# Three loads and one transposition moved along the queues of a fused sigmoid-attention and gated-FFN kernel

## The chip, the cores and the metric

The kernel runs on one core of a Trainium2 chip. The metric is the device time of one execution in microseconds (us). The time before is the median of three runs, 398.1 us (398.04 to 398.14).

## The reference

The inputs are `q`, `k` and `v` of shape (8 batches, 12 heads, 448 positions, 64) and three weight matrices. All are float32, and so is the output of 3584 rows of 768.

```python
scores = scale * np.matmul(q, k.transpose(0, 1, 3, 2)) - np.log(S)
attn = 1.0 / (1.0 + np.exp(-scores))          # a sigmoid, no sum over a row
x = np.matmul(attn, v)                        # then heads side by side: 3584 x 768
gate = np.maximum(x @ w_gate, 0.0)            # 768 -> 1536
out = (gate * (x @ w_val)) @ w_out            # 1536 -> 768
```

## The kernel before

**Tiling.** A batch has twelve heads, taken as three groups (g = 0, 1, 2) of four heads. The keys and queries of a group are held transposed in a tile `qkT`. The 448 positions are cut into seven chunks (c = 0 to 6). A *score unit* is one chunk of one group: `qk_unit` computes the scores on TensorE (L232) and their sigmoid on ScalarE (L187) into a tile `PT`. `pv_group` multiplies the seven `PT` tiles of a group by `v` (L250), and VectorE copies the result into `xT` (L184). The FFN of a batch follows: `gv` computes a gate block and a value block for each of twelve blocks f of 128 columns (L309), ScalarE or VectorE evicts the gate (L318, L320), and VectorE multiplies the two into `hT` (L327). Later FFN work is done for pairs of batches by sums of blocks (L385), which stay untouched.

**Order of TensorE.** It is written out by hand. Batches 1 to 7 have 21 score units each, cut into bursts m = 0, 1, 2 and so on. For batch 1 the bursts begin at units 0, 3, 6, 9, 13 and 17, and the `pv_group` of group 0 is in burst 3, that of group 1 in burst 5. The `pv_group` of group 2 stands in burst 0 of the next batch (`pv_finish`). Between bursts `ffn_mix(n)` takes n blocks off a queue of `gv` calls. During batch 1 these are still blocks of batch 0, whose positions are cut into two halves of 256 and 192: first the 192-wide blocks f = 0 to 5, then for f = 6 and 7, 8 and 9, 10 and 11 the 256-wide pair followed by the 192-wide pair.

**Loads.** `load` (L110), `load_v` (L114, L116), `load_gv` (L148) and `load_o` (L164) are all issued by GpSimd (POOL), one behind the other, and convert float32 to float16 on the way. Each transfer has one of eight semaphores in turn. A load so is not issued before the load eight places ahead of it has landed; the trace shows this as short POOL waits on DMAs. `k` and `q` of batches 2 to 7 share one buffer each, so the load of the next batch waits until the last group's copies (L215) have read the old one. `v` has two buffers in turn.

**Transposition.** Batches 0 and 1 are transposed on TensorE (`pe_transposes`, L201, L206). From batch 2 on `dma_transposes(b, g)` first has VectorE copy the group's `k` and `q` into a tile `rel` (L215, two instructions), and then SyncE (SP) issues a DMA transpose from `rel` to `qkT` (L219). `rel` has two buffers, so the third group's copies wait until the first group's transpose has landed. `qkT` has three.

**Where the changed steps stand.** `hold(b, g)` is a tiny copy on GpSimd (L646) that reads `qkT` of one group: POOL, and every load queued behind it, waits there until that transpose has landed. In burst 4 of batch 1 the first group of batch 2 is transposed; in burst 5, ahead of its two `gv` blocks, `late_loads` runs:

```python
4: [(3, lambda: dma_transposes(2, 0))],
5: [(2, late_loads)],
...
def late_loads():
    dma_transposes(2, 1)
    hold(2, 1)
    load_v(2)
    load_o()
```

The loads of batch 2's `k` and `q` are emitted in burst 0 of batch 1. Group 2 of batch 2 is transposed in burst 0 of batch 2, behind `pv_finish(1)`; in the same burst the loads of batch 3 are emitted. In the last burst of batch 2 the groups 0 and 1 of batch 3 are transposed, beside the first block of the down projection.

Of the kernel before, what the change touches and what calls it, by code (L numbers as in the profile page):

```python
# [17 lines left out]
def kernel(  # L18
# [75 lines left out]
    def tiles_of(b):  # L94
        if b not in in_tiles:
            pool = early if b == 1 else inp
            in_tiles[b] = tuple(
                p.tile([P, NPAIR, NCH * D], FP16, tag=t, name=t)
                for p, t in ((pool, "k16"), (pool, "q16"), (vinp, "v16"))
            )  # L100
        return in_tiles[b]

    def rows_of(src, b):
        return src[b].rearrange("(x r) (t c) d -> (r t) x (c d)", r=2, c=NCH)

    def load(b, g0, g1, which, c0=0, c1=NCH):
        for nm, t16, src in zip("kq", tiles_of(b), (k, q)):
            if nm in which:
                xs, cs = slice(2 * g0, 2 * g1), slice(c0 * D, c1 * D)
                nc.gpsimd.dma_start(t16[:, xs, cs], rows_of(src, b)[:, xs, cs])  # L110

    def load_v(b):
        v16 = tiles_of(b)[2]
        nc.gpsimd.dma_start(v16[:, 0::2, :], rows_of(v, b)[:, 0::2, :])  # L114
        for r in range(2):
            nc.gpsimd.dma_start(  # L116
                v16[64 - 64 * r : P - 64 * r, 1::2, :], rows_of(v, b)[64 * r : 64 * r + 64, 1::2, :]
            )
# [25 lines left out]
    def load_gv(f0, f1, which=(0, 1)):  # L144
        fs = slice(f0 * P, f1 * P)
        for i in which:
            wt, src = ((wg, moe_w_gate), (wv, moe_w_val))[i]
            nc.gpsimd.dma_start(wt[:, :, fs], src[:, fs].rearrange("(c p) f -> p c f", p=P))  # L148
# [6 lines left out]
    load(1, 0, 1, "kq")  # L155
    load_gv(6, 9)
    load(1, 1, 2, "kq")
    load_gv(9, 12)
    load_v(1)
    load(1, 2, 3, "kq")  # L160

    def load_o():
        for m0, m1 in ((0, 512), (512, DM)):
            nc.gpsimd.dma_start(  # L164
                wo[:, :, m0:m1], moe_w_out[:, m0:m1].rearrange("(c p) m -> p c m", p=P)
            )
# [23 lines left out]
    def qkT_of(b, g):  # L190
        if (b, g) not in qkT_tiles:
            qkT_tiles[(b, g)] = qkTp.tile([P, TW, P], FP16, tag="qkT", name="qkT")
        return qkT_tiles[(b, g)]
# [17 lines left out]
    def dma_transposes(b, g):  # L211
        k16, q16, _ = in_tiles[b]
        rel = relp.tile([P, TW, P], FP16, tag="rel", name="rel")
        for ti, t16 in enumerate((k16, q16)):
            nc.vector.tensor_copy(  # L215
                rel[:, ti * NCH : (ti + 1) * NCH, :].rearrange("p c (h d) -> p h c d", h=2),
                t16[:, 2 * g : 2 * g + 2, :].rearrange("p h (c d) -> p h c d", c=NCH),
            )
        nc.sync.dma_start_transpose(  # L219
            qkT_of(b, g)[:], rel[:].rearrange("p c x -> p (c x)")  # L220
        )
# [78 lines left out]
    def pv_group(b, g):  # L300
        pv(b, g, 0, S, [PT_tiles.pop((b, g, c))[:, :, 0:S] for c in range(NCH)])
# [66 lines left out]
    def open_late():  # L368
        first_sbuf.close()
        pool = ctx.enter_context(tc.tile_pool(name="late", bufs=1))  # L370
        late["T"] = pool.tile([P, 4, HF, HM], FP16, tag="T", name="T")
        late["X"] = pool.tile([P, 3, HD, S], FP16, tag="X", name="X")
        late["sums"] = ctx.enter_context(tc.tile_pool(name="sums", bufs=2))
# [21 lines left out]
    def weight_sums(i):  # L395
        T = [late["T"][:, j] for j in range(4)]
        B11, B21 = wo[:, 0:HF, 0:HM], wo[:, HF:NFC, 0:HM]
        B12, B22 = wo[:, 0:HF, HM:DM], wo[:, HF:NFC, HM:DM]
        sub(T[i], *((B12, B11), (B22, T[0]), (B22, B12), (B21, T[1]))[i])
# [96 lines left out]
    def batch_sums_t1(g):  # L496
        T1, _, _, B11, _, B12, _ = batch_blocks(g, (0, HD))
        sub(T1, B12, B11)

    def batch_sums(g, ks):  # L500
        T1, T2, T4, _, B21, B12, B22 = batch_blocks(g, ks)
        sub(B12, B22, B12)
        sub(T2, B22, T1)
        sub(T4, B21, T2)
# [132 lines left out]
    def pv_finish(b):  # L637
        pv_group(b, NG - 1)
        if b < 2:
            push_gv(b, 0, S, range(NFC))  # L640
# [4 lines left out]
    def hold(b, g):  # L645
        nc.gpsimd.tensor_copy(gate[0:1, :], qkT_tiles[(b, g)][0:1, 0, 0:2])  # L646

    def both(b, g):
        pe_transposes(b, g, 0)
        pe_transposes(b, g, 1)  # L650

    def late_loads():
        dma_transposes(2, 1)
        hold(2, 1)
        load_v(2)
        load_o()


# [2 lines left out]
    def push_group(g):  # L661
        tail = [("t", g, 6)] + [("y", g, p) for p in range(3)]
        if g == 0:
            tail.insert(0, tail.pop(1))
        work.extend([("w", g, f) for f in range(0, NFC, 2) if g > 0] + tail)
# [26 lines left out]
    for b in range(1, B):  # L692
        if b == 1:
            cuts, pv_at = (0, 3, 6, 9, 13, 17, 21), {3: (0, 2), 5: (1, 2)}
        elif b == 2:
            cuts, pv_at = (0, 4, 7, 11, 14, 18, 21), {0: (-1, 2), 2: (0, 2), 4: (1, 2)}
        else:
            cuts, pv_at = (0, 4, 8, 12, 16, 21), {0: (-1, 2), 2: (0, 2), 4: (1, 2)}
        count = len(cuts) - 1
        hooks = {}  # L700
        if b == 1:
            mix = (3, 3, 3, 3, 3, 2)
            hooks = {
                1: [(1, lambda: both(1, 1))],
                3: [(1, lambda: both(1, 2))],
                4: [(3, lambda: dma_transposes(2, 0))],
                5: [(2, late_loads)],
            }
        elif b == 2:
            mix = (2, 2, 1, 1, 1, 2)  # L710
            hooks = {
                2: [(0, prepare)],
                4: [(0, lambda: weight_sums(0))],
                5: [(1, lambda: weight_sums(1)), (0, lambda: weight_sums(2))],
            }
            open_late()
        elif b == 3:
            mix = (1, 1, 1, 0, 0)
        else:
            mix = (0,) * count  # L720
        for m in range(count):
            jobs = []
            for i, (g, c) in enumerate(order[cuts[m] : cuts[m + 1]]):
                if m in pv_at and i == pv_at[m][1]:
                    if m == 0:
                        pv_finish(b - 1)
                        if b == 2:
                            push_group(0)
                        elif b % 2 == 0:
                            push_group(b // 2 - 1)  # L730
                    else:
                        pv_group(b, pv_at[m][0])
                qk_unit(b, g, c)
            if m == 0 and b > 1:
                jobs.append(lambda: dma_transposes(b, 2))
            if b == 2 and m == count - 1:
                jobs.append(lambda: (dma_transposes(3, 0), dma_transposes(3, 1)))
            elif b == 3 and m == count - 1:
                jobs.append(lambda: (dma_transposes(4, 0), dma_transposes(4, 1)))
            elif 0 <= m - count + 2 and 3 < b < B - 1:  # L740
                jobs.append(lambda: dma_transposes(b + 1, m - count + 2))
            if b == 1:
                if m == 0:
                    load(2, 0, 1, "kq")
                    load(2, 1, 2, "kq")
                    load(2, 2, 3, "kq")
            elif m == 0 and b + 1 < B:
                if b == 3:
                    jobs.append(lambda: hold(3, 2))
                jobs.append(lambda: (load(b + 1, 0, 3, "kq"), load_v(b + 1)))  # L750
            if b % 2 and b > 2:
                if m == count - 1:
                    jobs.append(lambda: (batch_sums_t1(b // 2), batch_sums(b // 2, (0, 1))))
            elif b > 3 and m == 0:
                jobs.append(lambda: batch_sums(b // 2 - 1, (1, HD)))
            if b == 2 and m == count - 1:
                ffn_mix(mix[m], hooks[m])
                next_work(jobs + [lambda: weight_sums(3)], first_act=True)
            elif mix[m]:
                for job in jobs:  # L760
                    job()
                ffn_mix(mix[m], hooks.get(m, ()))
            else:
                next_work(jobs)
            if b == 3 and m in (1, 3):
                for f in range(*((0, 8, 2), (8, NFC, 2))[m // 2]):
                    gate_sums(f, f + 2)
# [35 lines left out]
```

## Time and profile before

| what | value |
|---|---|
| median of three runs | 398.1 us (398.04 to 398.14) |
| the profiled execution | 399.14 us |
| its span | 397.3 us |
| TensorE (PE) busy | 388.5 us, 98% of the span |
| ScalarE (ACT) busy | 223.2 us, 56% |
| VectorE (DVE) busy | 279.6 us, 70% |
| GpSimd (POOL) busy | 49.5 us, 12% |
| granted TensorE clock | 1.0 |

The span is the time from the first to the last instruction of the profiled execution; 1.84 us of that execution lie around it. Times in the views count from the start of the span. PE is the matrix engine, PEld its weight loads. The timeline merges like instructions that follow each other: a line gives the start, the length, the engine, the source line, the operation with its tiles, and a count; in brackets stands the idle time before it and what ended it. Successive matmuls overlap in the record, since their ends are modelled, so the distance between the starts of two lines says better than their lengths how long the first kept the engine.

### The profile page before, as it was taken

What the parts mean: (1) busy time and instruction counts of PE and PEld (TensorE: products, weight loads), DVE (VectorE), ACT (ScalarE), POOL (GpSimd) and SP (SyncE); (2) the same over time, 40 slices, a digit from 0 to 9 for tenths busy, and PEclk for the clock granted to TensorE, in tenths of its full rate; (3) what the DMA queues carried; (4) which work ended last, traced back from release to release, by engine and by line L of the source; (5) the groups of instructions that cost most, each with busy time, mean ns of one, the idle gap of its engine ahead of it and who ended that gap; (6) DMA issues with size and microseconds to landing.
All of it is one profiled execution on the core that took longest, in us unless ns stands there. A gap on an engine that the chain in (4) does not pass through costs nothing.

```text
span 397.3 us, 8744 instructions
## 1 busy us (share of the span) xinstructions
PE 388.5 (98%) x3488; PEld 217.5 (55%) x3488; DVE 279.6 (70%) x539; ACT 223.2 (56%) x476; POOL 49.5 (12%) x73
## 2 busy tenths in 40 slices
PE   8999999999999999999999999999999999999995
PEld 3678686445455554554555555455455555555563
DVE  3453345358377889999758889999776779987662
ACT  5946768684785565655665455565566233543121
POOL 8643400700030300003000300000000000000000
PEclk9999999999999999999999999999999999999999
DMA  9999994999999893224945695222013320000135
GB/s 150 196 198 204 206 129 87 180 203 190 203 143 180 167 218 53 46 48 54 177 84 133 130 219 89 48 21 57 19 40 81 81 79 2 0 1 2 40 94 146
DMA packets 68953, 43.69 MB, mean 110 GB/s; under 512 B 35888, under 2 KB 65584, under 8 KB 68912
## 3 DMA queue, kind: packets, MB, share of 16 engines
q0 software_dynamic: 30736, 23.33, 39.2%
q1 hardware_dynamic: 37744, 19.34, 23.2%
q8 instruction: 27, 0.44, 0.4%
q10 hardware_dynamic: 432, 0.46, 0.4%
q14 instruction: 14, 0.11, 0.1%
HBM read 47.19 MB, written 11.01 MB: 146 GB/s over the span
## 4 chain that ended last, share of the span: by engine, by line
PE 84%; DMA 11%; POOL 2%; ACT 1%; issue 0%; DVE 0%; ACTq 0%; POOLq 0%; DVEq 0%
PE u L385 32%; PE g L385 15%; PE y L385 8%; PE qk_ps L232 7%; PE pv_ps L250 7%; PE g_ps L309 5%; PE v_ps L309 5%; DMA wg<-in_moe_w_gate_dram 4%; DMA v<-in_v_dram 3%; PE ya L346 3%; DMA q<-in_q_dram 2%; PE yb L346 1%; DMA qkT<-rel 1%; ACT PT L187 1%; POOL k L110 1%; POOL q L110 1%
## 5 line engine op out<-in xcount | busy, mean ns | idle before, releaser
L187 ACT ACTIVATE PT<-qk_ps 128x448 f16<-128x448 f32 (+3 forms) x318 | 150.5, 595 | 72.6 <-PE qk_ps L232 72.5
L385 PEld LDWEIGHTS <-S 128*128 128x128 f16 x540 | 52.8, 98 | 43.6
L536 DVE TENSOR_TENSOR gsb<-g,gsb 128x448 f32<-128x448 f32 x72 | 42.9, 625 | 14.6 <-PE g L385 14.1
L232 PE MATMUL qk_ps<-qkT 64*64 64x448 f16 (+2 forms) x756 | 49.9, 336 | 1.3 <-DVE qkT L206 0.5
L421 ACT ACTIVATE ysb<-u 128x384 f32<-128x384 f32 x27 | 13.4, 498 | 53.4 <-PE u L385 53.4
L327 DVE TENSOR_TENSOR hT<-gate_sb,v_ps 128x256 f16<-128x256 f32 (+2 forms) x36 | 16.2, 465 | 34.7 <-ACT gate_sb L318 22.3
L532 ACT COPY gsb<-u 128x448 f32<-128x448 f32 x48 | 25.7, 566 | 23.9 <-PE u L385 22.9
L250 PE MATMUL pv_ps<-PT,v 64*64 64x448 f16 (+2 forms) x756 | 37.7, 329 | 1.1 <-DMA v<-in_v_dram 0.8
L184 DVE TENSOR_SCALAR xT<-pv_ps 128x448 f16<-128x448 f32 (+2 forms) x53 | 27.9, 567 | 15.2 <-PE pv_ps L250 13.8
L385 PEld LDWEIGHTS <-hT 128*128 128x128 f16 x288 | 27.7, 98 | 19.8 <-issue 2.1
L232 PEld LDWEIGHTS <-qkT 64*64 64x64 f16 x756 | 20.0, 105 | 25.5 <-issue 16.3
L309 PE MATMUL v_ps<-xT,wv 128*128 128x256 f16 (+2 forms) x216 | 33.3, 290 | 0.3 <-DMA wv<-in_moe_w_val_dram 0.3
L309 PE MATMUL g_ps<-xT,wg 128*128 128x256 f16 (+2 forms) x216 | 33.5, 291 | 0.1
L385 PEld LDWEIGHTS <-wv 128*128 128x128 f16 x216 | 21.1, 98 | 19.7
L385 PEld LDWEIGHTS <-wg 128*128 128x128 f16 x216 | 20.3, 98 | 20.6 <-issue 3.0
L250 PEld LDWEIGHTS <-v 64*64 64x64 f16 x756 | 21.8, 107 | 12.8 <-DMA v<-in_v_dram 1.5
L385 PE MATMUL u<-T,hT 128*128 128x384 f16 x144 | 27.3, 326 | 0.0
L437 DVE SCALAR_TENSOR_TENSOR ysb<-y,ysb 128x384 f32<-128x384 f32 x24 | 13.4, 557 | 17.8 <-PE y L385 10.3
L309 PEld LDWEIGHTS <-wg 128*128 128x128 f16 x216 | 18.5, 98 | 11.5 <-issue 5.0
L110 POOL DMA_DIRECT2D k<-in_k_dram x14 | 10.9, 780 | 110.7 <-DVE rel L215 104.4
L309 PEld LDWEIGHTS <-wv 128*128 128x128 f16 x216 | 20.1, 98 | 7.9 <-DMA wv<-in_moe_w_val_dram 0.6
L385 PE MATMUL u<-xT,wg 128*128 128x448 f16 x108 | 23.5, 353 | 0.1
(69 smaller groups left out, 531.0 us busy)
## 6 DMA issues: line engine op xcount, KB each, us to landing
out_dram<-ysb SPq DMA_DIRECT2D x52, 192.0 KB, 3.0
k<-in_k_dram POOLq DMA_DIRECT2D x5, 672.0 KB, 11.7
q<-in_q_dram POOLq DMA_DIRECT2D x5, 672.0 KB, 14.9
v<-in_v_dram POOLq DMA_DIRECT2D x8, 336.0 KB, 15.4
v<-in_v_dram POOLq DMA_DIRECT2D x16, 168.0 KB, 15.2
k<-in_k_dram POOLq DMA_DIRECT2D x8, 224.0 KB, 10.4
wo<-in_moe_w_out_dram POOLq DMA_DIRECT2D x1, 1536.0 KB, 13.1
q<-in_q_dram POOLq DMA_DIRECT2D x6, 224.0 KB, 11.3
```

The source lines that it names most:

```text
L110: nc.gpsimd.dma_start(t16[:, xs, cs], rows_of(src, b)[:, xs, cs])
L184: nc.vector.tensor_scalar(out=xT, in0=src, scalar1=XSCALE, scalar2=None, op0=AOP.mult)
L187: nc.scalar.activation(PT_ap, ps_ap, AF.Sigmoid, bias=sig_bias, scale=qk_scale)
L232: nc.tensor.matmul(out_of(hh)[o : o + 64, :], qkT[rows, c, cols], qkT[rows, NCH + c0 : NCH + c1, cols], start=True, stop=True, tile_positi ...
L250: nc.tensor.matmul(ps[hh][64 * r : 64 * r + 64, 0:qn], v16[rows, 2 * g + hh, c * D : (c + 1) * D], pieces[c][rows, hh, :], start=(c == 0), ...
L309: nc.tensor.matmul(ps[-1][:, 0:qn], wt[:, dc, f * P : (f + 1) * P], xT_tiles[b][:, dc, q0 : q0 + qn], start=(dc == 0), stop=(dc == NDC - 1),)
L327: nc.vector.tensor_tensor(out=hT_tiles[g][:, f, o : o + qn], in0=gate_sb[:, 0:qn], in1=ps[1][:, 0:qn], op=AOP.mult,)
L346: nc.tensor.matmul(ps[:, 0 : m1 - m0], hT_tiles[g][:, f, t * P : (t + 1) * P], wo[:, f, m0:m1], start=(f == 0), stop=(f == NFC - 1),)
L385: nc.tensor.matmul(ps[:, 0:n], A[:, k_, :], W[:, k_, :], start=(first and k_ == 0), stop=(k_ == kn - 1), skip_group_check=True,)
L421: nc.scalar.activation(o, ps[:, 0:HM], AF.Copy, scale=OUT_SCALE)
L532: by(gs[u][i][:], ps[u][:, 0:S])
L536: nc.vector.tensor_tensor(out=gs[u][i][:], in0=ps[u][:, 0:S], in1=gs[u][i][:], op=AOP.add)
```

## The change

Three things move. The loads of batch 1's `v` (three transfers) are issued ahead of the last quarter of the gate and value weights (two transfers, blocks f = 9 to 11) instead of behind them. The loads of batch 2's `v` (three transfers) are issued directly behind its `k` and `q`, ahead of `hold(2, 1)`, instead of behind it. And the transposition of batch 2's group 2 (two VectorE copies and one DMA transpose) is emitted directly behind that of group 1, in burst 5 of batch 1, instead of in burst 0 of batch 2. Nothing is added or taken away.

```diff
@@ -155,8 +155,8 @@
     load(1, 0, 1, "kq")
     load_gv(6, 9)
     load(1, 1, 2, "kq")
+    load_v(1)
     load_gv(9, 12)
-    load_v(1)
     load(1, 2, 3, "kq")
@@ -651,8 +651,8 @@
     def late_loads():
         dma_transposes(2, 1)
+        dma_transposes(2, 2)
         hold(2, 1)
-        load_v(2)
         load_o()
@@ -731,7 +731,7 @@
-            if m == 0 and b > 1:
+            if m == 0 and b > 2:
                 jobs.append(lambda: dma_transposes(b, 2))
@@ -744,6 +744,7 @@
                     load(2, 0, 1, "kq")
                     load(2, 1, 2, "kq")
                     load(2, 2, 3, "kq")
+                    load_v(2)
```

## Prediction

> **What bounds the kernel now.** I read the page first: TensorE is busy 98% of the span at a granted clock of 1.0 throughout, so time can come only from the few places where it stands still, or from making new ones. The view of waits, kept to TensorE, names two such places behind DMAs after the start-up: `pv_ps` for `v` (0.8 us) and `qk_ps` for `qkT` (0.4 us). The timeline of TensorE shows the first, and further down the same burst of work without a wait:
>
> ```profile
> 46.78 0.57 PE L232 MATMUL qk_ps<-qkT 64*64 64x448 f16 x8
> 47.18 0.35 PE L250 MATMUL pv_ps<-PT,v 64*64 64x448 f16 x2
> 47.83 0.37 PE L250 MATMUL pv_ps<-PT,v 64*64 64x448 f16 x1 [0.29 <-DMA v<-in_v_dram]
> 48.69 1.51 PE L250 MATMUL pv_ps<-PT,v 64*64 64x448 f16 x25 [0.49 <-DMA v<-in_v_dram]
> 49.85 0.72 PE L232 MATMUL qk_ps<-qkT 64*64 64x448 f16 x8
> ...
> 59.95 0.57 PE L232 MATMUL qk_ps<-qkT 64*64 64x448 f16 x8
> 60.36 1.49 PE L250 MATMUL pv_ps<-PT,v 64*64 64x448 f16 x28
> 61.68 0.55 PE L232 MATMUL qk_ps<-qkT 64*64 64x448 f16 x8
> ```
>
> From the start of the 28 `pv` matmuls to the scores behind them it is 49.85 - 47.18 = 2.67 us in batch 1's first group, 61.68 - 60.36 = 1.32 us in its second. The bracketed 0.78 us understates the loss, which is 1.35 us. The second place:
>
> ```profile
> 99.77 1.14 PE L385 MATMUL u<-T,hT 128*128 128x384 f16 x6
> 101.36 0.57 PE L232 MATMUL qk_ps<-qkT 64*64 64x448 f16 x8 [0.45 <-DMA qkT<-rel]
> ```
>
> Six matmuls of this shape take 0.975 us from start to start in the rows above it, so the scores of batch 3 could begin at 100.75; they begin at 101.36. The loss is 0.61 us.
>
> The timeline of POOL gives the order of the loads. The load view, asked for one issue at a time, adds the time to landing.
>
> ```profile
> 26.34 0.84 POOL L148 DMA_DIRECT2D wg<-in_moe_w_gate_dram  x1 [1.27 <-DMA wg<-in_moe_w_gate_dram]
> 28.30 0.82 POOL L148 DMA_DIRECT2D wv<-in_moe_w_val_dram  x1 [1.12 <-DMA wv<-in_moe_w_val_dram]
> 29.44 0.74 POOL L114 DMA_DIRECT2D v<-in_v_dram  x1 [0.32 <-DMA k<-in_k_dram]
> 30.62 0.63 POOL L116 DMA_DIRECT2D v<-in_v_dram  x1 [0.44 <-DMA q<-in_q_dram]
> 34.91 0.63 POOL L116 DMA_DIRECT2D v<-in_v_dram  x1 [3.66 <-DMA wg<-in_moe_w_gate_dram]
> ...
> 48.94 0.71 POOL L110 DMA_DIRECT2D q<-in_q_dram  x1
> 69.35 0.17 POOL L646 COPY gate<-qkT 1x2 f16<-1x2 f16 x1 [19.70 <-DMA qkT<-rel]
> 69.83 0.76 POOL L114 DMA_DIRECT2D v<-in_v_dram  x1 [0.31 <-issue]
> ```
>
> The last `v` of batch 1 lands 13.7 us after 34.91, at 48.65: TensorE resumes at 48.69. The loads land in their order, one behind the other: `q` before the last weights at 39.44 (24.36 + 15.1), the weights at 42.3 and 45.2, `v` at 48.65, batch 1's last `k` and `q` at 49.7 and 50.9, batch 2's last `q` at 57.6. So `v` costs the queue 3.4 us and the two weight loads 5.8 us.
>
> **Part 1, batch 1's `v` first.** Bytes and order up to batch 1's last `k` and `q` are otherwise the same, so `v` lands at 39.4 + 3.4 = 42.9, well before 47.18, and the 1.35 us go. What pays are the weights, now at 42.9 + 5.8 = 48.7 for the value half and 45.8 for the gate half. The first user is block f = 9 of the first half: gates at 51.83, values at 52.49, less the 1.35 us by which TensorE is now early, so 50.48 and 51.14. That leaves 2.5 us for the later one: no cost. Batch 1's last `q`, unchanged at 50.9, is transposed on TensorE after 53.65 - 1.35 = 52.3, its `k` (49.7) from 51.9. The eight semaphores move by the permutation alone and still leave eight loads in flight. ScalarE and VectorE, idle 1.37 and 2.75 us behind the old wait, start as early as TensorE lets them. **Gain 1.35 us**, from 1.0 (if a bank is not free at once) to 1.35.
>
> **Part 2, batch 2's `v` at 50 instead of 70.** On POOL the three issues follow `q` of 48.94; their semaphores' older loads land by 52, and the buffer (batch 0's) was last read at 31. POOL has nothing else to do until its hold. `v` lands at 57.6 + 3.4 = 61.1, is needed at 76.85, and has no price there. Its price is contention: the DMA transpose of (2, 0) was issued at 56.46, as the load queue ran dry (DMA share 0.21 in 56 to 58 by the windows view), and landed in 5.1 us, at 61.55. It is now issued at 55.11 (its sources landed by 53.1) with `v` still on the engines. Bounds from the same line's rows: 3.9 us alone (at 162.84), 12.2 us with a whole batch's loads beside it (at 133.77). About 1.55 us of each is SP's own instruction, so its moving takes 2.4 us alone and 10.7 beside loads, a share of 0.22. Loads run roughly 1.7 us ahead of their landings (57.6 against a dry queue at 56), so at 56.7 about 2.8 us of `v` remain; slowed to three quarters (what that share leaves them), they end at 60.3. By then the transpose has done 0.22 x 3.7 = 0.8 of its 2.4 us. It finishes at 61.9, or at 63.0 with the 1.15 us that this execution of (2, 0) took beyond the quiet row. I take the middle, 62.4. Below 61.1 I see no way, above 63.2 little, because the whole of `v` is only 3.4 us of work.
>
> A rule bears on this. The Trainium skill, "DMA: Bandwidth & Descriptors", section "Queues, rings and completion order", says that each DMA engine goes round-robin, a packet at a time, among the queues that have work, so the transposition would get an equal turn against `v`. Taken as half of the time that would be my estimate from the page: 61.5, or 62.6 with the same 1.15; the 0.22 measured beside loads decides here, and the two sums differ by little.
>
> **Part 3, group 2's transposition one burst sooner.** VectorE gets two copies of 0.3 us in a new place:
>
> ```profile
> 62.96 0.38 DVE L215 COPY rel<-k 128x896 f16<-128x896 f16 x1
> 63.26 0.39 DVE L215 COPY rel<-q 128x896 f16<-128x896 f16 x1
> 64.24 0.62 DVE L327 TENSOR_TENSOR hT<-gate_sb,v_ps 128x192 f16<-128x192 f32 x2 [0.59 <-ACT gate_sb L318]
> ```
>
> They fit into the 0.59 us that VectorE spends waiting for ScalarE (63.56, 63.86, then `hT` at 64.2), so by themselves they cost nothing. But they wait for the landing of (2, 0), whose `rel` buffer they overwrite. With the advance VectorE arrives at 63.56 - 1.35 = 62.2. Behind it stand these `hT` products, which free the PSUM banks of the `pv_group` that TensorE starts at 64.65 - 1.35 = 63.3: there is no slack, so every us of landing after 62.2 is lost once. At 62.4 that is 0.2, with two copies' spacing **0.3 us**; bounds 0 and 1.0. TensorE itself needs (2, 0) for its scores at 64.25 - 1.35 = 62.9, later than VectorE does. On SP the DMA transpose of (2, 2) follows (2, 1); the next behind it is that of (3, 0), at 96.75. It is needed at 84.09, and landed in 4.0 us before.
>
> **Part 4, what moves behind the hold.** Without `v` ahead, `w_out` and batch 3's loads go out about 2 us earlier from POOL and, 3.4 us of transfers lighter, land 4 to 5 us earlier. The copies that batch 3's `k` must wait for are done by then. VectorE's position, not the loads, sets the copies of (3, 0) at 96.00. But the transpose issued at 96.75 shared the engines with batch 3's `v` (last landing 77.0 + 22.4 = 99.4) and took 4.6 us; with `v` landing near 95 it should take 3.9 to 4.1 as at 105.11, 162.84 and 173.59, against the 4.0 that TensorE leaves it. **Gain 0.55 us** of the 0.61; the bounds are 0.61 and a loss of 1.0 (the longest row without loads, at 63.72, took 5.6).
>
> **The sum.** 1.35 - 0.3 + 0.55 = 1.6 us. From there to the end no gap of TensorE longer than 0.12 us is left, so the advance is kept. The profiled execution takes 399.14 us, span and 1.84 around it, 1.0 over the median; I take the same 1.6 off both: 397.5 for a profiled execution, **396.5 us** for the median. About 0.2%, 0.8 us, is what a measurement can tell from no change.
>
> **The rivals.** *Slower:* the transpose of (2, 0) stays behind `v` as at 133.77. It would land at 55.1 + 12.2 = 67.3, VectorE and TensorE would lose 5.1 us, and the time would be 398.1 + 5.1 - 1.9 = 401.3. It decides from a landing after 62.2 + 1.9 = 64.1. For it speak three rows of 10.6 to 12.2 us; against it that those had about 13 us of loads beside them, and here there are three. Chance 0.11, mostly at 398.9 to 400. *No change:* another wait takes the place of the first, either the late value weights (if the loads run 2.5 us behind their old pace) or batch 1's last `q` (1.4 us of slack); or (2, 0) lands near 63.2 and (3, 0) gains nothing. That leaves 0 to 0.8: about 397.7. Chance 0.13. *Only the first:* batch 3's wait stays, and the gain is 1.05: 397.0, chance 0.2.
>
> **How the numbers follow.** The forecast has 0.56. It and the case of the first wait alone are faster by over 0.2%: 0.76. Within it 0.13, slower 0.11. The low end is both waits gone at no price, 1.35 + 0.61 = 1.96 us and a little spread: 395.9. The high end takes in most of the no-change case: 397.9.
>
> **What would show it.** Right: the 28 `pv` of 47.18 in one line with scores 1.32 us later; `wv` without a wait at L309; the (2, 0) transpose issued near 55.1, with a landing of 6.5 to 7.5 us; scores of batch 3 near 99.1 with no bracket. Wrong: a bracket `DMA qkT` or an idle VectorE near 62, or a longer `rel` wait; then part 2's share was mis-sized.

## The result and the profile after

The changed kernel takes 397.35 us (median of 13 runs, 397.05 to 398.14) beside 398.14 us of the kernel before (13 runs). The ratio is 0.9979, 95% interval 0.9971 to 0.9986: 0.8 us, or 0.2%, faster, half of the 1.6 us forecast. A second comparison gave 0.9979 again (0.997 to 0.9988). The profiled execution of the changed kernel, however, is 2.1 us shorter than that of before: 397.06 us against 399.14, spans 395.3 and 397.3. The profiles therefore show more than the timed runs gained, and most of what follows is about this difference.

The timeline of TensorE in the changed kernel, at the two places where it waited before:

```profile
46.79 0.57 PE L232 MATMUL qk_ps<-qkT 64*64 64x448 f16 x8
47.19 1.49 PE L250 MATMUL pv_ps<-PT,v 64*64 64x448 f16 x28
48.51 0.55 PE L232 MATMUL qk_ps<-qkT 64*64 64x448 f16 x8
...
98.25 1.14 PE L385 MATMUL u<-T,hT 128*128 128x384 f16 x6
99.35 0.57 PE L232 MATMUL qk_ps<-qkT 64*64 64x448 f16 x8
```

The 28 `pv` matmuls stand in one line, with the next scores 1.32 us behind them. The scores of batch 3 start 1.10 us behind the last down product; 0.975 is the product itself, so 0.12 us of the old 0.61 are left. The POOL timeline of the same kernel shows the three moves:

```profile
25.62 0.76 POOL L114 DMA_DIRECT2D v<-in_v_dram  x1 [1.24 <-DMA wg<-in_moe_w_gate_dram]
28.27 1.26 POOL L116 DMA_DIRECT2D v<-in_v_dram  x2 [1.89 <-DMA wv<-in_moe_w_val_dram]
30.00 0.86 POOL L148 DMA_DIRECT2D wg<-in_moe_w_gate_dram  x1 [0.47 <-DMA q<-in_q_dram]
32.88 0.82 POOL L148 DMA_DIRECT2D wv<-in_moe_w_val_dram  x1 [2.02 <-DMA wg<-in_moe_w_gate_dram]
...
48.73 0.76 POOL L114 DMA_DIRECT2D v<-in_v_dram  x1 [0.66 <-PE pv_ps L250]
...
67.99 0.17 POOL L646 COPY gate<-qkT 1x2 f16<-1x2 f16 x1 [16.56 <-DMA qkT<-rel]
69.06 2.07 POOL L164 DMA_DIRECT2D wo<-in_moe_w_out_dram  x2 [0.90 <-issue]
```

Batch 1's `v` has landed by 41.8 and the value weights by 47.1; nobody waits for either. Behind the hold `w_out` goes out directly, 2.9 us earlier than before, and batch 3's `q` lands at 91.4 instead of 95.8. VectorE around the moved transposition:

```profile
62.04 0.39 DVE L215 COPY rel<-k 128x896 f16<-128x896 f16 x1
62.35 0.39 DVE L215 COPY rel<-q 128x896 f16<-128x896 f16 x1
62.72 0.62 DVE L327 TENSOR_TENSOR hT<-gate_sb,v_ps 128x192 f16<-128x192 f32 x2
```

There is no bracket on the copies of (2, 2): the transpose of (2, 0), issued at 54.95, took 6.6 us and landed at 61.56, half a microsecond ahead of them.

### The profile page after: what moved, and what is told of

Read it like the earlier page. It is cut to its first block, busy times and chain, and to the rows that moved or that the text cites. A ratio compares the mean times of both kernels' runs of the same rounds, so it can differ in the third digit from the quotient of the medians.

```text
span 395.3 us, 8744 instructions
## 1 busy us (share of the span) xinstructions
PE 387.6 (98%) x3488; PEld 217.6 (55%) x3488; DVE 279.5 (71%) x539; ACT 223.0 (56%) x476; POOL 49.4 (13%) x73
## 4 chain that ended last, share of the span: by engine, by line
PE 94%; ACT 3%; DMA 1%; DVE 1%; issue 0%; ACTq 0%; DVEq 0%
PE u L385 33%; PE g L385 16%; PE qk_ps L232 9%; PE y L385 9%; PE pv_ps L250 8%; PE g_ps L309 8%; PE v_ps L309 7%; PE ya L346 3%; ACT PT L187 2%; PE yb L346 1%; PE trt L201 1%; DMA ysb<-in_q_dram 1%; DVE qkT L206 0%; PE warm_ps L175 0%; ACT ysb L421 0%
## 5 line engine op out<-in xcount | busy, mean ns | idle before, releaser
L250 PE MATMUL pv_ps<-PT,v 64*64 64x448 f16 (+2 forms) x756 | 36.9, 329 | 0.7 <-issue 0.7
```

Source lines behind the costliest of these rows:

```text
L250: nc.tensor.matmul(ps[hh][64 * r : 64 * r + 64, 0:qn], v16[rows, 2 * g + hh, c * D : (c + 1) * D], pieces[c][rows, hh, :], start=(c == 0), ...
```

## The experiments

The theories were these. **A:** the pace of the load queue differs from execution to execution, and the first profile of before showed a slow one, so the wait for `v` is usually shorter than 1.35 us. **B:** the waits are as in that profile every time. **C:** the gain is given back by the transposition of (2, 0) and its copies. **G:** the advance is lost again later, where VectorE waits for batch 3's `q`.

**The kernel before, again** (no edit), against itself, and a third profiled execution of it:

> The kernel before, once more, for a second profile and a null comparison. Theory A (the load queue's pace differs from execution to execution, and the first profile of before was a slow one): the last v of batch 1 lands clearly earlier than the 48.65 us of the first profile, about 47.0 to 47.5, the loss around the pv matmuls of 47.18 is under 0.6 us instead of 1.5, and the span is nearer 396.4 than 397.3. Theory B (the waits of the first profile are there in every execution): v lands at 48.4 to 48.9, the loss is 1.3 to 1.5 us, the span 397.1 to 397.5. Ratio to the kernel before 1.000 within 0.1% by both.

> The kernel before, a third profile. Theory A: the landing of batch 1's last v varies between 47.5 and 48.7 from execution to execution, and the loss around the pv matmuls goes with it, one for one, from 0.3 to 1.5 us; the loss at the scores of batch 3 is 0.5 to 0.8 us. Theory B: 1.3 to 1.5 us for v.

The ratio is 1.0005 (0.9997 to 1.0014), which says how small a difference can be told. The profiled executions took 399.34 and 398.56 us, and the last `v` landed at 48.54 and 47.97. TensorE's timeline in the second and in the third:

```profile
47.43 0.77 PE L250 MATMUL pv_ps<-PT,v 64*64 64x448 f16 x3
48.58 1.51 PE L250 MATMUL pv_ps<-PT,v 64*64 64x448 f16 x25 [0.38 <-DMA v<-in_v_dram]
49.74 0.72 PE L232 MATMUL qk_ps<-qkT 64*64 64x448 f16 x8
...
47.42 0.36 PE L250 MATMUL pv_ps<-PT,v 64*64 64x448 f16 x3
48.01 1.51 PE L250 MATMUL pv_ps<-PT,v 64*64 64x448 f16 x25 [0.23 <-DMA v<-in_v_dram]
49.17 0.72 PE L232 MATMUL qk_ps<-qkT 64*64 64x448 f16 x8
```

From the first `pv` to the scores it is 2.31 us in the second and 1.75 us in the third, losses of 0.99 and 0.43 against 1.35 in the first. Two things vary: the landing, and how late TensorE is already (its scores ahead of these `pv` began at 46.78, 47.03 and 47.01). While TensorE waits for `v` it does not matter when it came there. B, the same wait every time, is refuted. A's numbers were too low for the second profile, whose `v` landed where B had it (48.4 to 48.9), and right for the third.

**Batch 1's `v` alone**, two comparisons and one more profile:

```diff
+    load_v(1)
     load_gv(9, 12)
-    load_v(1)
```

> Batch 1's v ahead of the last gate and value weights, and nothing else of the change. Theory A: in its profile the pv matmuls run in one line of 1.32 us, but against the runs of before it gains only what a typical execution of before loses there, 0.2 to 0.5 us (397.7 to 397.9). Theory B: 1.3 to 1.5 us gained (396.7). Both: the wait for the transpose of (3, 0) near 99.5 us stays, 0.4 to 0.6 us.

> Batch 1's v alone, once more, beside the changed kernel on the same chip: the first time it gained 0.14 us in the timed runs, where its profile shows 1.4 to 1.5 less wait than that of before. Theory A (a typical execution of before hardly waits for v): 0.1 to 0.5 us under before, again, and 0.5 to 0.9 over the changed kernel. Theory B: 1.3 under before, the first measurement an accident. Theory G (the advance is lost again 50 us later, where VectorE then waits for the landing of batch 3's q): the profile shows q of batch 3 landing after VectorE's copies of (3, 0) could start, near 94.5, and scores of batch 3 0.8 us or more late.

> Batch 1's v alone, a third profile. In two profiles TensorE lost 0.5 and 0.7 us at the scores of batch 3 and the times were 397.5 and 397.8, but half of its timed runs stand near 398.4. Theory A with a load queue at the edge: this profile is again at 397.4 to 397.9, or, if it shows the slow half, VectorE's copies of (3, 0) wait for batch 3's q, or the scores of batch 3 come 1.2 us late. By theory B neither.

Ratios 0.9994 (0.9986 to 1.0003) and 0.9993 (0.9984 to 1.0002): 0.1 to 0.4 us by the medians, not the 1.3 of theory B. In all three profiles (397.51, 397.82, 398.20 us) the 28 `pv` run without a wait, and the scores of batch 3 lose 0.52, 0.70 and 0.71 us, as in before (0.61, 0.74, 0.76). The third profile is 0.4 to 0.7 us longer than the others because it reached the `pv` 0.5 us later (47.70): a start-up wait for batch 0's `v` near 16 us that nothing absorbs any more. Theory G asked for a later `q` and 0.8 us or more; `q` landed at 94.2 to 94.9 and the losses stayed below, so G does not explain it.

The second and the first of these profiles also lose 0.18 and 0.07 us at a place that the prediction had priced at nothing, the first `pv` of batch 2: its `v` lands at 75.43 and 75.33, and the `pv` start at 75.30 and 75.31. The second profile of before loses 0.26 there (76.94 against 76.74). In the first, on which the prediction rests, that `v` came 0.08 us early. With batch 2's `v` moved it lands some 15 us ahead of its use.

**Batch 2's `v` and the transposition, without batch 1's `v`** (the other three hunks of the diff):

> Batch 2's v behind its k and q, and group 2's transposition one burst sooner; batch 1's v stays behind the last weights. Theory A: the wait for the transpose of (3, 0) goes, about 0.5 us gained (397.6), the transpose of (2, 0) takes 6 to 7 us beside v and nobody waits for it. Theory B: 0.5 us gained too. Rival C (the missing part of the gain is given back by contention: (2, 0) or the two copies stop VectorE in typical runs): no gain or a loss here, 398.1 to 398.8, while batch 1's v alone gives 1.3.

Ratio 0.9985 (0.9976 to 0.9994), 397.88 us. The loss at the scores of batch 3 fell to 0.12, that for `v` was 0.61 in this execution. C, which wanted a loss here, falls as the explanation. Beside the 397.38 us of the kernel below, measured in the same comparison, and the changed kernel's 397.35 and 397.44 it says that batch 1's `v` is worth about 0.5 us once the other wait is gone. That is an estimate: the intervals of the ratios overlap.

**Both loads moved, the transposition left:**

```diff
+    load_v(1)
     load_gv(9, 12)
-    load_v(1)
...
         hold(2, 1)
-        load_v(2)
...
                     load(2, 2, 3, "kq")
+                    load_v(2)
```

> Both loads of v moved, group 2's transposition left in burst 0 of batch 2. Tells whether moving the transposition matters: by my sum it only removes a chance of VectorE waiting for the landing of (2, 0) at 62.0, so this kernel should have the time of the whole change (397.35) within 0.2 us by theories A and B; by rival C it is faster than the whole change by 0.3 us or more.

397.38 us, 0.9975 (0.9967 to 0.9984): the whole change's time. Moving the transposition is worth nothing measurable.

**The changed kernel, again:**

> The changed kernel once more, for a second profile and a second interval. All theories: 0.9979 of before within 0.1%, the pv matmuls of 47.2 in one line, no wait at the scores of batch 3. By theory A its profile is at 396.9 to 397.6, since nothing in it hangs on the pace of the loads; the transpose of (2, 0) lands at 61.3 to 62.1.

397.44 us. The profiled execution took 397.75 us, 0.7 more than the first and outside what was expected, and shows what the first did not, on VectorE and then on TensorE:

```profile
62.79 0.39 DVE L215 COPY rel<-k 128x896 f16<-128x896 f16 x1 [0.68 <-DMA qkT<-rel]
...
63.80 1.51 PE L250 MATMUL pv_ps<-PT,v 64*64 64x448 f16 x26 [0.33 <-DVE hT L327]
```

The transpose of (2, 0) took 7.75 us here and landed at 62.67. VectorE's copies of (2, 2) waited 0.68 us, the `hT` products behind them came late, and the `pv_group` waited for their PSUM banks; the scores of batch 3 are 0.68 us later than in the first profile at the same start. This is the price that the sum put at 0.3, by the path that the prediction named: nothing in one execution, 0.7 in the other.

What made the landing 1.1 us later is not more loads beside it. The view of the DMA queues, kept to 59.4 to 60.9, gives packets, MB and a busy share; `software` are GpSimd's loads, `hardware` is the transpose:

```profile
q1 hardware_dynamic: 171, 0.04, 66.6%
q0 software_dynamic: 14, 0.01, 5.1%
```

The loads are as good as through, and the transpose moves 171 packets, where the first execution moved 1177 in the same stretch. A standstill of this kind stands in before too, with no load left: 17 packets from 58.6 to 59.6. In all three a fetch of instructions (one transfer of 16 KB on queue q8) runs at its start or just ahead of it: 58.84 to 59.73, 58.13 to 59.03 in the first execution with a shorter standstill, 57.86 to 59.12 in before. That the fetch causes it is not shown.

**The price doubled:** the second part of `w_out` also goes ahead of the hold.

```diff
                     load_v(2)
+                    load_o(((512, DM),))
...
         hold(2, 1)
-        load_o()
+        load_o(((0, 512),))
```

> The changed kernel with the second part of w_out (4.0 us of transfers) also loaded ahead of the hold, behind batch 2's v: the load queue now ends near 64 instead of 60. It doubles the suspected price of part 2. Prediction's mechanism (the transpose of (2, 0) has a fifth of the engines while loads run, and VectorE's copies of (2, 2), from 62.0 on, wait for its landing): (2, 0) lands at 63.5 to 65.5, VectorE and then TensorE lose 1.3 to 3 us, and the time is 398.5 to 400. Rival (the transpose does not suffer from loads that were queued before it, or has slack of several us): within 0.3 us of the changed kernel.

404.09 us, 1.0141 (1.0125 to 1.0156), far beyond the 398.5 to 400 expected. TensorE and VectorE in its timeline:

```profile
68.15 0.96 PE L232 MATMUL qk_ps<-qkT 64*64 64x448 f16 x8 [4.83 <-DMA qkT<-rel]
...
68.23 0.39 DVE L215 COPY rel<-k 128x896 f16<-128x896 f16 x1 [5.58 <-DMA qkT<-rel]
```

The transpose of (2, 0) took 12.6 us and landed at 68.11, just behind the last load at 67.73. Four microseconds of loads more (they took 6.0 beside the transpose) moved its landing by 5.4 to 6.6 us, not by the two or three expected. The DMA queues show how. From 55.4 to 59.4 they move 1065 packets of loads and none of the transpose. From 61.5 to 64.0 it is

```profile
q0 software_dynamic: 594, 0.30, 87.6%
q1 hardware_dynamic: 600, 0.15, 46.5%
```

so the two take turns packet for packet, and a packet of the transpose is half as large here (256 bytes against 512). That is 240 packets per microsecond; alone it moves about 810 (1210 from 164.0 to 165.5 in before). The transpose starts late and then runs at three tenths of its speed while loads last. The slower rival's mechanism is real, and the changed kernel's two landings, 61.56 and 62.67, lie on either side of its threshold, the copies that VectorE could start at 62.04.

**Late `q` without the neighbouring load:** batch 3's `v` ahead of its `k` and `q`.

```diff
-                jobs.append(lambda: (load(b + 1, 0, 3, "kq"), load_v(b + 1)))
+                if b == 2:
+                    jobs.append(lambda: (load_v(3), load(3, 0, 3, "kq")))
+                else:
+                    jobs.append(lambda: (load(b + 1, 0, 3, "kq"), load_v(b + 1)))
```

> The changed kernel with batch 3's v loaded ahead of its k and q, so that q lands 3.4 us later, near 94.8 instead of 91.4, about when VectorE copies it (94.5 to 94.8), and no load is left when (3, 0) is transposed. It brings back the late q of before without the neighbouring load. Theory G: 0.5 to 0.9 us slower than the changed kernel in the timed runs, a wait of 0.2 to 0.6 in the profile. If instead the load beside the transpose was what cost TensorE its 0.6 us in before: within 0.2 us of the changed kernel, the transpose at 3.9 to 4.1.

397.71 us, 0.9985 (0.9975 to 0.9994), 0.27 over the changed kernel: between the two expectations. In the profile `q` landed at 95.11 and held VectorE for 0.08 us; the transpose took 4.06 and the scores lost 0.20. With `v` behind `q`, as in before and in batch 1's `v` alone, it took 4.5 to 4.7 and they lost 0.5 to 0.8. So most of that loss goes when no load is beside the transpose, and the late `q` makes a little. One rival stands: in the eight slow rows of this transpose a 16 KB fetch of instructions ends 0.3 to 1.4 us after its issue, in the six quick ones 0.8 us or more ahead of it. No run parts the fetch from the load.

**Two attempts at a better kernel.** Both hold batch 2's `v` back until (2, 0) has landed; the second also puts the copies of (3, 0) ahead of the third weight sum.

```diff
-                4: [(3, lambda: dma_transposes(2, 0))],
+                4: [(3, lambda: (dma_transposes(2, 0), hold(2, 0), load_v(2)))],
...
                     load(2, 2, 3, "kq")
-                    load_v(2)
```

```diff
-                5: [(1, lambda: weight_sums(1)), (0, lambda: weight_sums(2))],
+                5: [(1, lambda: weight_sums(1)), (0, lambda: (dma_transposes(3, 0), weight_sums(2)))],
...
-                jobs.append(lambda: (dma_transposes(3, 0), dma_transposes(3, 1)))
+                jobs.append(lambda: dma_transposes(3, 1))
```

> The changed kernel, but batch 2's v is loaded behind a hold on the transpose of (2, 0) in burst 4, so that the two no longer share the engines; it then runs beside the transpose of (2, 1), which nobody needs before 75. My theory of the price of part 2 (none in one profile of the changed kernel, 0.7 us in the other): (2, 0) lands in 4.6 to 5.3 us, VectorE never waits near 62, and the median is 0.2 to 0.4 us below the changed kernel's, 397.0 to 397.2. Rival: the spread of the changed kernel's times has another cause; then the median stays at 397.4.

> As v2_held, and the transposition of (3, 0) stands ahead of the third weight sum on VectorE, 1.3 us sooner, for its q has landed by 92. The last 0.12 us at the scores of batch 3 go, and a slow transpose there has 1.2 us of slack: 396.8 to 397.1, the fastest. If the third weight sum, now 0.6 us later, holds up the product that reads it: 0.2 us or more slower than v2_held.

Both missed: 398.37 us (0.9992, 0.9983 to 1.0001) and 398.18 us (0.9994, 0.9983 to 1.0004), no better than before. The POOL timeline of the first, and the scores of batch 3:

```profile
60.97 0.17 POOL L646 COPY gate<-qkT 1x2 f16<-1x2 f16 x1 [11.63 <-DMA qkT<-rel]
61.45 0.76 POOL L114 DMA_DIRECT2D v<-in_v_dram  x1 [0.31 <-PE qk_ps L232]
62.20 1.27 POOL L116 DMA_DIRECT2D v<-in_v_dram  x2
71.67 0.17 POOL L646 COPY gate<-qkT 1x2 f16<-1x2 f16 x1 [8.20 <-DMA qkT<-rel]
72.95 2.07 POOL L164 DMA_DIRECT2D wo<-in_moe_w_out_dram  x2 [1.11 <-issue]
...
100.66 0.57 PE L232 MATMUL qk_ps<-qkT 64*64 64x448 f16 x8 [0.74 <-DMA qkT<-rel]
```

(2, 0) landed in 5.4 us, a little over the 4.6 to 5.3 expected, and VectorE did not wait for it near 62. But `v` now ran beside the transpose of (2, 1), which took 8.8 us, and the hold behind `v` waits for just that one. `w_out` went out at 72.95 instead of 69.06, `q` of batch 3 landed at 95.5, and the scores of batch 3 lost 0.90 us. I had asked who needs `qkT` of (2, 1) on TensorE and forgot the hold. In the second the scores lost only 0.09, but VectorE met the late `q` earlier (0.31 us), and the product just ahead of the scores began 0.18 us late, at 99.49: VectorE, delayed, had read that product's old bank only by 99.44. So in this profile the edit gains nothing. TensorE also reached the `pv` of batch 1 at 48.24, the latest of all.

No kernel beat the changed one; leaving the transposition where it was ties with it.

## Why the prediction was right or wrong

All fourteen profiles can be laid side by side, because from the first scores of batch 3 to the end of the span every one of them takes 295.93 to 296.00 us. All differences arise ahead of that point. Losses in us:

| kernel | scores ahead of the `pv` at | loss at `v` | price of (2, 0) | loss at batch 3's scores |
|---|---|---|---|---|
| before, three profiles | 46.78, 47.03, 47.01 | 1.35, 0.99, 0.43 | 0, 0, 0 | 0.61, 0.74, 0.76 |
| batch 2's `v` and transposition | 46.77 | 0.61 | 0 | 0.12 |
| batch 1's `v` alone, three | 46.76, 46.76, 47.30 | 0, 0, 0 | 0, 0, 0 | 0.52, 0.70, 0.71 |
| changed, two | 46.79, 46.77 | 0, 0 | 0, 0.68 | 0.12, 0.12 |

**Right.** The direction, and the time lies in the range. The mechanism of each part is seen in the profiles. The late gate and value weights cost nothing: 47.07 landed, 50.97 needed. `v` of batch 2 lands at 60.11, where 61.1 was forecast. The transpose of (2, 0) lands at 61.56 and 62.67, where 61.9 to 63.0 was forecast, and its price of 0.3 us is near the mean of 0 and 0.68. Part 4's 0.55 us is 0.49 against the first profile of before, 0.58 as a mean. The second wait went, with `v` of batch 3 out of the way, as argued; the fetch named above stays a rival for the cause.

**Right in part by luck: the landing of (2, 0).** The sum let it move from 1.55 us behind its issue on, at 56.7, and the loads end at 60.3. SP's own instruction took 2.43 and 3.07 us, no packet moved before 57.4, and few loads were left by 59.4; the two errors offset each other.

**Wrong: the size of part 1.** Its 1.35 us came from a single execution. That wait is set by the pace of 47 us of loads on one side and by TensorE's start-up on the other, and in the four profiles with the old order it was 0.43 to 1.35, 0.85 in the mean. The first profile had both the latest `v` and almost the earliest TensorE. A further 0.18 us that I did not count went with the wait, at the scores just behind it. The wait also covered whatever TensorE had lost before it, and that comes to light once it is gone. In the profiles of kernels with batch 1's `v` moved the scores ahead of the `pv` begin anywhere from 46.76 to 47.84, though TensorE's work up to there is the same in all, and these delays go straight into the time. In two of the late ones (47.30 with the transposition left, 47.84) the time is lost at one `pv` near 23 us, where the profile names no releaser (0.89 and 1.19 us). The lower bound of 1.0 which I gave to this gain should have been near 0.1. In timed runs the other parts gave 0.5 us (398.37 to 397.88), where the sum had 0.55 - 0.3 = 0.25, so all that is missing from the 1.6 is missing from part 1.

**Not settled.** That the wait varies is shown in the profiles, but they do not add up to the timed runs. The three profiled executions of before lie at 399.14, 399.34 and 398.56 us, above the timed medians of 398.1 to 398.4, those of the other kernels within about 0.7 of theirs on both sides. A mean loss of 0.85 + 0.18 in the profiles stands against 0.1 to 0.4 us that batch 1's `v` alone gained in timed runs, and about 0.5 with the other part in place. Part of this gap is what the wait covered: counted by position, the scores behind the `pv` begin at 49.47 in the mean of the four profiles with the old order and at 48.84 in the ten with the new, 0.63 us apart and not 0.85. For the rest, either timed executions of before have an earlier `v` or a later start than profiled ones; timed runs leave no timeline, and the experiments don't tell these apart.

The Trainium skill ("DMA: Bandwidth & Descriptors", section "Issuing engines are not separate DMA queues") says that transfers issued by different engines run on the same DMA engines and interleave. The runs agree: 4.0 us for a transpose alone, 12.6 beside loads. Its round robin, which the prediction quotes, fits the trace as a count of packets, 594 against 600 above. It does not fit as half of the time: in the kernel with the price doubled that would have put (2, 0) at 55.46 + 1.55 + 4.8 = 61.8, and it landed at 68.11. The 0.22 from the rows of before gives 55.46 + 1.55 + 2.4 / 0.22 = 67.9 and was the better guide.

## What to carry to other kernels

A wait in one profile is one draw from several. Where it lies between a queue of transfers and an engine whose arrival also varies, compare several executions before its length is put into a sum, and ask which earlier delays it covers. When a transfer is moved, list every instruction that waits for what it will collide with, tiny holds on a queue included. Here a load moved from behind a hold to ahead of it paid, one moved behind an earlier hold undid it, and four microseconds of transfers too many ahead of it cost 6.7.

## What I had not expected of the hardware

A DMA transpose with a queue of loads beside it starts late (its first packet moves 2.6 us after its issue in the changed kernel and 4.1 with the price doubled, 1.2 in a quick row) and then gets every second packet, not half of the time (issue to landing 3.9 to 4.1 us in its quick rows, 6.1 to 7.8 with the tail of one `v`, 12.6 with 4 us of loads more). Even with no load beside it a row can take 5.1 to 5.6 us, with a standstill of about 1 us in its packets. And TensorE's start-up differs between executions of the same instructions by up to 1.1 us (the scores at 46.76 to 47.84), while the 296 us behind it repeat to 0.07 us.
